# A spectral mixer on one core: single x tiles and a gated constant load in front, filter rows interleaved for one multiply per unit

## The chip, the cores and the metric

The kernel runs on one core of one Trainium2 chip. The metric is the time of the whole kernel on the device in microseconds, median of the runs. A profile of one execution comes with it; its span is a little shorter than the time (134.2 us against 136.11 us), since it leaves out what lies around the first and last instruction.

## The reference

Two blocks follow each other on x, 2048 by 512 in bf16. The first normalises x, takes a two-dimensional real Fourier transform, multiplies by a complex filter `w_r + i w_i` (2048 by 257), and transforms back. The second normalises again and applies a token-mixing MLP over the 2048 rows.

```python
def _A_ref(x, w_r, w_i):
    X = rfft2(x.astype(float32), axes=(-2, -1))
    X = X * (w_r + 1j * w_i)
    return irfft2(X, s=(S, D), axes=(-2, -1)).astype(bfloat16)

def _B_ref(x, w1, b1, w2, b2):
    h = _layernorm(x, axis=-1)
    u = gelu(einsum("bsd,sf->bdf", h, w1) + b1)      # F = 1376
    return (einsum("bdf,fs->bds", u, w2) + b2).transpose(0, 2, 1)

h  = x + _A_ref(_layernorm(x), A_w_r, A_w_i)
h2 = h + _B_ref(_layernorm(h), B_w1, B_b1, B_w2, B_b2)
```

## The kernel before

Row `16*p + s2` of x lies in partition `p` as tile `s2`, so x is 16 tiles of 128 by 512. The stages are:

1. front: statistics of each tile, first DFT matrices `FP` scaled by the tile's `1/std` into `FS` (so the normalisation is folded into the transform), matmuls `f1` on x, eviction to `Y`;
2. filter, in eight units `u` of four groups: `f2` (transform along the columns) to `CS`, `x` (the rest of the row transform) to PSUM, the multiply `v` by the filter rows `W` to `V`, and `g1` (start of the inverse) to `PQ`;
3. the rest of the inverse (`g2`, `g3`), the residual (`TT`, `H`), the second normalisation (`HH`);
4. the MLP, `mm1`, gelu and `mm2`.

A unit's multiply needs the `W` rows of its chunk: chunk 0 serves unit 0, chunk 1 units 1 to 3, chunk 2 units 4 to 7.

The instructions aren't written in order by hand. Each is declared with its engine, a priority and an assumed duration, and a list scheduler in Python picks the order for every engine before the program is built:

```python
st = max(eng_free[o.stream], o.dep_ready, avail, o.not_before)
key = (st, -o.prio, o.idx)          # earliest start first, then the higher priority
...
if o.is_dma:
    x0 = max(st + (3200.0 if st < 4000.0 else 1700.0), dma_free)
    dma_free = x0 + o.bytes / o.rate
    o.finish = dma_free + 200.0
```

The loads of the front, on the sync queue (SP) unless `"act"` is given, and the warm-up of TensorE:

```python
for q, (a, b) in enumerate(((0, 2), (2, 4), (4, 6), (6, 8), (8, 12))):
    ldx(a, b, 90 - q)               # x tiles a to b-1, 128 KB each
ldf(2, 84)                          # 4 tiles of FP, 256 KB
ldx(12, 16, 83)
ldf(3, 82)
ldf(0, 90, "act")
act("table", ..., ACT.Abs_reciprocal_sqrt, ..., prio=88)
ldf(1, 87, "act", 1800.0)
dma("ld_E", ...); dma("ld_MR", ...) # constants of the later stages
...
K.op("zt", "dve", lambda eng, bank: eng.memset(ZT[:, :], 0.0), ..., prio=60)
for w_ in range(N_WARM):            # N_WARM = 20, matmuls on zeros
    warm(f"warm{w_}", wu, 50, first=w_ == 0, occ=427.0 if w_ < 9 else 216.0)
# matmuls f1 have prio 14; 12 more warm matmuls (prio 13) stand after the first tiles
```

The statistics of tiles 1 and 3 are on ScalarE, those of the others on VectorE (`bn_stats`, `bn_aggr`). The scaling `FS` of nine tiles is on GpSimd, the rest on ScalarE and VectorE.

The filter rows and the multiply:

```python
add("W", [NP, 2, NG, LW], bf, rw)   # partition, w (real or imaginary), group, 257 columns
...
d = W[0:NP:2, w, g0:g0 + ng, :].rearrange("p g l -> p (g l)")      # plus rows, both components
dma(f"ld_wp{ch}_{w}", d, AP(dram, g0 * LW, [[64 * LW, 32], [0, 2], [1, ng * LW]]), ...)
for comp in range(2):                                             # minus rows, one component
    d = W[1 + 2 * comp::4, w, h0:h0 + nh, :]
    dma(f"ld_wm{ch}_{w}{comp}", d, AP(dram, (64 - h0) * LW, [[64 * LW, 32], [-LW, nh], [1, LW]]), ...)
# chunk 0 has one more transfer for each w; ld_w1 waits for the last load of chunk 2
...
for w in range(2):                  # stage_x, unit u; ng groups, nh = 2 in units 0 and 7
    wt  = W[:, w, g0 + h * ng:g0 + h * ng + ng, :]
    win = AP(wt, wt.offset + 1, [.., [LW, ng], [1, 2], [2, NP]])
    vout = V[:, g0 + h * ng:g0 + h * ng + ng, w, :]
    eng.tensor_tensor(vout, psum, win, ALU.mult)
```

Of the kernel before, what the change touches and what calls it, by code (L numbers as in the profile page):

```python
# [36 lines left out]
def _row(sign, comp, k2, s):  # L37
    return 4 * (k2 * 2 + s) + 2 * comp + sign
# [136 lines left out]
class Builder:  # L175
# [101 lines left out]
    def schedule(self):  # L277
# [14 lines left out]
        while len(order) < len(ops):  # L292
# [38 lines left out]
            if o.is_dma:  # L331
                x0 = max(st + (3200.0 if st < 4000.0 else 1700.0), dma_free)
                dma_free = x0 + o.bytes / o.rate
                o.finish = dma_free + 200.0
            else:
                o.finish = st + o.lat
# [86 lines left out]
def memory_layout():  # L423
# [26 lines left out]
    add("W", [NP, 2, NG, LW], bf, rw)  # L450
# [21 lines left out]
    add("tb", [NP, 8], f32, region(32))  # L472
    add("B1s", [NP, 16], bf, region(32))
# [17 lines left out]
def build_kernel(nc, A_x, A_w_r, A_w_i, B_w1, B_b1, B_w2, B_b2, out):  # L491
# [68 lines left out]
    def ldf(q, pr_, stream="sp", nb=0.0):  # L560
        sl = slice(4 * q, 4 * q + 4)
        dma(f"ld_FP{q}", FP[:, sl, :, :], cin["FP"][:, sl, :, :], 1 << 18, outs=[FP[:, sl, :, :]], prio=pr_, stream=stream, not_before=nb)

    for q, (a, b) in enumerate(((0, 2), (2, 4), (4, 6), (6, 8), (8, 12))):
        ldx(a, b, 90 - q)
# [3 lines left out]
    ldf(0, 90, "act")  # L569
    act("table", T["tb"][:, 0:1], EPS[:, 0:1], ACT.Abs_reciprocal_sqrt, 1, ins=[EPS[:, 0:1]], prio=88)  # L570
    ldf(1, 87, "act", 1800.0)
# [3 lines left out]
    for ch, (u0, u1) in enumerate(((0, 1), (1, 4), (4, 8))):  # L575
        g0, ng = 4 * u0, 4 * (u1 - u0)
        lst = []
        for w, dram in ((0, A_w_r), (1, A_w_i)):
            d = W[0:NP:2, w, g0:g0 + ng, :].rearrange("p g l -> p (g l)")
            lst.append(dma(f"ld_wp{ch}_{w}", d, bass.AP(dram.tensor, g0 * LW, [[64 * LW, 32], [0, 2], [1, ng * LW]]),  # L580
                           64 * ng * 514, prio=42 - ch, group=f"w{ch}"))
            h0, nh = (g0, ng) if g0 else (1, ng - 1)
            for comp in range(2):
                d = W[1 + 2 * comp::4, w, h0:h0 + nh, :]
                lst.append(dma(f"ld_wm{ch}_{w}{comp}", d, bass.AP(dram.tensor, (64 - h0) * LW, [[64 * LW, 32], [-LW, nh], [1, LW]]),
                               32 * nh * 514, prio=42 - ch, group=f"w{ch}", rate=300.0))
            if g0 == 0:
                d = W[1:NP:2, w, 0, :]
                lst.append(dma(f"ld_wz{ch}_{w}", d, bass.AP(dram.tensor, 32 * LW, [[64 * LW, 32], [0, 2], [1, LW]]),
                               64 * 514, prio=42 - ch, group=f"w{ch}", rate=300.0))  # L590
# [21 lines left out]
    ZT, BV = T["ZT"], T["bv"]  # L612
    K.op("zt", "dve", lambda eng, bank: eng.memset(ZT[:, :], 0.0), outs=[ZT[:, :]], occ=200.0, prio=60)  # L613
# [98 lines left out]
    def stage_x(u):  # L712
# [14 lines left out]
        for h in range(nh):  # L727
            for w in range(2):
                wt = W[:, w, g0 + h * ng:g0 + h * ng + ng, :]
                win = bass.AP(wt.tensor, wt.offset + 1, [list(wt.ap[0]), [LW, ng], [1, 2], [2, NP]])  # L730
                vout = V[:, g0 + h * ng:g0 + h * ng + ng, w, :].rearrange("p g (y j) -> p g y j", y=2)

                def tt(eng, bank, h=h, win=win, vout=vout):
                    s = psf[:, bank * 512 + h * 512:bank * 512 + h * 512 + 256 * ng].rearrange("p (g y j) -> p g y j", g=ng, y=2)
                    return eng.tensor_tensor(vout, s, win, ALU.mult)  # L735
                K.op(f"v_{u}_{h}{w}", "dve", tt, ins=[wt], outs=[vout], occ=50.0 + 1065.0 / nh, lat=170.0 + 1065.0 / nh, unit=unit, pr=True,
                     last=h == nh - 1 and w == 1, prio=11, after=wload[u])
# [93 lines left out]
    K.emit(es, ["dq_st"] + [f"dq_st_{s2}" for s2 in range(NS2 - 2, NS2)])  # L831
# [45 lines left out]
```

## Time and profile before

| what | before |
|---|---|
| time, median of 3 runs | 136.11 us (136.06 to 136.16) |
| span of the profile | 134.2 us |
| TensorE busy | 124.3 us, 93% |
| VectorE busy | 69.8 us, 52% |
| ScalarE busy | 63.9 us, 48% |
| GpSimd busy | 12.1 us, 9% |
| bytes moved | 22.16 MB in 12808 packets, 2592 of them under 512 B and 8736 under 2 KB |

In the profile PE is TensorE's matmuls and PEld its weight loads, DVE is VectorE, ACT ScalarE, POOL GpSimd. SPq and ACTq are the issues of transfers from the sync and the scalar engine. `L527` is the line of a helper that records every matmul, so matmuls are told apart by the tiles they read (`FS,X` is `f1`, `EM,Y` is `f2`, `CS,EM` is `x`, `EM,V` is `g1`). The chain of waits is followed back from the last instruction, at each step to what released it; time on it is what the end depends on. A row of the timeline has the start in us, the duration, the engine and the instruction, and in brackets how long the engine was idle before it and what it waited for. Rows of the timeline are merged, so one can hold several instructions (its `x` count).

### The profile page before, as it was taken

The numbers are of one execution on the slowest core, as the hardware profiler recorded it, in microseconds if no ns is written. First come the engines' busy times: TensorE is split into PE (matmuls) and PEld (weight loads), VectorE is DVE, ScalarE is ACT, GpSimd is POOL, SyncE is SP. The second block draws the span as 40 slices with busy tenths as digits, with TensorE's granted clock in tenths as the row PEclk, the third lists the DMA queues.
The fourth block names the chain that finished last, engine by engine and source line by source line (L and its number), as shares of the span: only waits on it lengthen the run. The fifth ranks groups of instructions, "written<-read, shape, count | busy, mean of one in ns | idle before, by whom it ended". The sixth has DMA issues, their size and how long they took to land.

```text
span 134.2 us, 2017 instructions
## 1 busy us (share of the span) xinstructions
PE 124.3 (93%) x776; PEld 74.4 (55%) x786; DVE 69.8 (52%) x137; ACT 63.9 (48%) x146; POOL 12.1 (9%) x33
## 2 busy tenths in 40 slices
PE   6979989998976979999999999999999999999991
PEld 2436656676845835654434444446666666666660
DVE  0379966999693799999981000000233242332422
ACT  4479976968955999995779622222000000000000
POOL 0198800006000000000000000000000000000000
PEclk9999999999999999999999999999999999999999
DMA  3999999989999999910000000000011212112121
GB/s 79 359 388 389 348 342 346 322 238 433 421 433 402 404 415 261 336 50 5 0 0 0 0 0 0 5 0 0 12 66 39 78 39 69 53 39 78 39 76 41
DMA packets 12808, 22.16 MB, mean 165 GB/s; under 512 B 2592, under 2 KB 8736, under 8 KB 12160
## 3 DMA queue, kind: packets, MB, share of 16 engines
q1 hardware_dynamic: 12512, 21.52, 45.0%
q10 hardware_dynamic: 288, 0.52, 1.4%
q8 instruction: 6, 0.10, 0.3%
q14 instruction: 2, 0.02, 0.0%
HBM read 19.95 MB, written 2.10 MB: 164 GB/s over the span
## 4 chain that ended last, share of the span: by engine, by line
PE 59%; DVE 24%; ACT 8%; DMA 5%; issue 1%; SPq 1%; ACTq 0%
PE ps L527 59%; DVE H L795 7%; ACT Y L545 5%; DMA X<-in_A_x_dram 5%; DVE TT L786 4%; DVE TT L788 4%; DVE HH L800 4%; DVE V L735 4%; ACT rs L545 1%; ACT PQ L545 1%; ACT FS L545 1%; DVE st L649 1%; SPq L517 1%; DVE OUT L825 1%; PE ps L617 0%
## 5 line engine op out<-in xcount | busy, mean ns | idle before, releaser
L527 PE MATMUL ps<-HH,W 128*128 128x512 bf16 (+1 forms) x173 | 40.4, 380 | 1.3 <-DVE HH L800 0.9
L527 PE MATMUL ps<-GT,W 128*128 128x512 bf16 (+1 forms) x172 | 37.9, 379 | 0.2
L825 DVE SCALAR_TENSOR_TENSOR OUT<-ps,B2f,H 128x512 bf16<-128x512 f32 x16 | 12.0, 751 | 48.7 <-PE ps L527 48.7
L527 PEld LDWEIGHTS ps<-GT,W 128*128 128x128 bf16 (+1 forms) x176 | 25.4, 144 | 12.7
L527 PEld LDWEIGHTS ps<-HH,W 128*128 128x128 bf16 (+1 forms) x176 | 17.2, 100 | 21.3 <-DVE HH L800 1.9
L735 DVE TENSOR_TENSOR V<-ps,W 128x1024 bf16<-128x1024 f32 (+1 forms) x20 | 18.5, 1001 | 1.9 <-PE ps L527 1.9
L545 ACT ACTIVATE GT<-ps,B1f 128x512 bf16<-128x512 f32 (+1 forms) x11 | 7.1, 688 | 14.6 <-PE ps L527 14.6
L545 ACT ACTIVATE JK<-H,nm 128x512 bf16<-128x512 bf16 x16 | 11.6, 724 | 3.0 <-DVE H L795 2.9
L527 PE MATMUL ps<-EM,V 128*128 128x128 bf16 x128 | 10.8, 220 | 1.2 <-DVE V L735 1.2
L649 DVE BATCH_NORM_STATS2 st<-X 128x6 f32<-128x512 bf16 x14 | 9.2, 666 | 5.1 <-DMA X<-in_A_x_dram 5.1
L545 ACT ACTIVATE PQ<-ps 128x512 bf16<-128x512 f32 x16 | 9.1, 596 | 4.3 <-PE ps L527 3.9
L617 PE MATMUL ps<-ZT 128*128 128x512 bf16 x32 | 9.4, 430 | 1.6 <-DVE ZT L613 1.2
L795 DVE TENSOR_TENSOR H<-ps,TT 128x512 bf16<-128x512 f32 x16 | 10.9, 683 | 0.0
L527 PE MATMUL ps<-EM,Y 128*128 128x256 bf16 x64 | 9.4, 274 | 0.7 <-ACT Y L545 0.4
L527 PEld LDWEIGHTS ps<-EM,V 128*128 128x128 bf16 x128 | 7.8, 98 | 3.9 <-DVE V L735 1.9
L527 PE MATMUL ps<-EM,PQ 128*128 128x256 bf16 x64 | 9.0, 273 | 0.8 <-ACT PQ L545 0.7
L545 ACT ACTIVATE EO<-ps 128x512 bf16<-128x512 f32 x16 | 9.2, 598 | 0.9 <-PE ps L527 0.9
L545 ACT ACTIVATE CS<-ps 128x512 bf16<-128x512 f32 x15 | 8.5, 602 | 2.3 <-PE ps L527 2.3
L527 PE MATMUL ps<-FS,X 128*128 128x256 bf16 x64 | 8.4, 274 | 1.0 <-POOL FS L629 0.8
L629 POOL TENSOR_SCALAR FS<-FP,rs 128x256 bf16<-128x256 bf16 x9 | 8.3, 935 | 0.9 <-ACT rs L545 0.9
L786 DVE TENSOR_TENSOR TT<-ps,X 128x256 f32<-128x256 f32 x16 | 6.7, 419 | 3.2 <-PE ps L527 3.2
L527 PEld LDWEIGHTS ps<-FS,X 128*128 128x128 bf16 x64 | 5.6, 97 | 4.1 <-POOL FS L629 2.6
(36 smaller groups left out, 79.6 us busy)
## 6 DMA issues: line engine op xcount, KB each, us to landing
W<-in_B_w_dram SPq DMA_DIRECT2D x4, 1376.0 KB, 11.4
W<-in_B_w_dram SPq DMA_DIRECT2D x10, 512.0 KB, 16.5
out_dram<-OUT SPq DMA_DIRECT2D x16, 128.0 KB, 1.7
X<-in_A_x_dram SPq DMA_DIRECT2D x4, 256.0 KB, 5.7
X<-in_A_x_dram SPq DMA_DIRECT2D x2, 512.0 KB, 7.5
EM<-c_EM SPq DMA_DIRECT2D x3, 256.0 KB, 8.3
W<-in_A_w_r_dram SPq DMA_DIRECT2D x1, 514.0 KB, 5.7
W<-in_A_w_r_dram SPq DMA_DIRECT2D x2, 257.0 KB, 6.2
```

The source lines that it names most:

```text
L517: return eng.dma_start(dst, src)
L527: return K.op(name, "pe", lambda eng, bank: eng.matmul(outf(bank), lhsT, rhs, start=start, stop=stop), ins=ins or [lhsT, rhs], occ=occ, la ...
L545: return eng.activation(dst, s, func, **kw)
L617: return K.op(name, "pe", lambda eng, bank: eng.matmul(ps[:, bank, :], ZT[:, 0:NP], ZT[:, :], start=True, stop=True), ins=[ZT[:, :]], occ= ...
L629: dve(f"fs{i}", lambda eng, bank: eng.tensor_scalar(FS[:, i, :, :], FP[:, i, :, :], rs, None, op0=ALU.mult), [FP[:, i, :, :], rs], [FS[:, ...
L649: dve(f"st_{i}", lambda eng, bank, i=i, x=x: eng.bn_stats(ST[:, i, 0:6], x), [x], [ST[:, i, 0:6]], 512, prio=25)
L735: return eng.tensor_tensor(vout, s, win, ALU.mult)
L786: dve(f"tl_{s2}", lambda eng, bank, tt=tt, xl=xl: eng.tensor_tensor(tt[:, 0, :], ps[:, bank, 256:512], xl, ALU.add), [xl], [tt[:, 0, :]], ...
L788: dve(f"th_{s2}", lambda eng, bank, tt=tt, xh=xh: eng.tensor_tensor(tt[:, 1, :], xh, ps[:, bank, 256:512], ALU.subtract), [xh], [tt[:, 1, ...
L795: return eng.tensor_tensor(hs.rearrange("p (h d) -> p h d", h=2), e, tt[:, :, :], ALU.add)
L800: dve(f"hh_{s2}", lambda eng, bank, s2=s2, hs=hs: eng.tensor_scalar(HH[:, s2, :], hs, NM[:, s2:s2 + 1], R2[:, s2:s2 + 1], op0=ALU.add, op1 ...
L825: dve(f"fin{s2}", lambda eng, bank, dst=dst, bia=bia, hs=hs: eng.scalar_tensor_tensor(dst, ps[:, bank, :], bia, hs, op0=ALU.add, op1=ALU.add),
```

## The change

The change has three parts.

The front: x tiles 0 and 1 come as single transfers of 128 KB, the later ones in pairs; the first DFT rows (`ld_FP0`) are issued only after a gate, a clear of a scratch tile on VectorE that does nothing else; the second DFT rows move from the scalar queue to the sync queue; and a transfer of 64 bytes out of the DFT constants is issued at once. It's meant to bring the first x tile sooner, with nothing beside it on the way.

The filter rows: `W` is laid out with real and imaginary rows of a group side by side, and the rows of a unit's partitions are reordered so that the component is the fastest index. Every transfer then carries rows of one component, 514 bytes at a time, in place of the plus rows of both components at once.

The multiply: with that layout one instruction multiplies PSUM, read twice, by both the real and the imaginary rows.

The scheduler's model of a transfer is changed with it, so the order of instructions may differ in other places too.

```diff
 def _row(sign, comp, k2, s):
-    return 4 * (k2 * 2 + s) + 2 * comp + sign
+    return 4 * (k2 * 2 + s) + 2 * sign + comp
...
-                x0 = max(st + (3200.0 if st < 4000.0 else 1700.0), dma_free)
-                dma_free = x0 + o.bytes / o.rate
+                x0 = max(st + (1750.0 if st < 900.0 else 2200.0), dma_free)
+                dma_free = x0 + o.bytes / (min(o.rate, 310.0) if x0 < 7000.0 else o.rate)
...
-    add("W", [NP, 2, NG, LW], bf, rw)
+    add("W", [NP, NG, 2, LW], bf, rw)
...
-    for q, (a, b) in enumerate(((0, 2), (2, 4), (4, 6), (6, 8), (8, 12))):
-        ldx(a, b, 90 - q)
+    gate = K.op("gate", "dve", lambda eng, bank: eng.memset(T["TT0"][:, :, :], 0.0), outs=[T["TT0"][:, :, :]], occ=560.0, prio=59)
+    for q, (a, b) in enumerate(((0, 1), (1, 2), (2, 4), (4, 6))):
+        ldx(a, b, 96 - q)
+    ldf(1, 88)
+    ldx(6, 8, 87)
+    ldx(8, 10, 86)
+    ldx(10, 12, 85)
     ldf(2, 84)
     ldx(12, 16, 83)
     ldf(3, 82)
-    ldf(0, 90, "act")
-    act("table", ..., prio=88)
-    ldf(1, 87, "act", 1800.0)
+    act("table", ..., prio=95)
+    dma("touch", T["pt"][0:1, :], cin["FP"][0:1, 0, 0, 0:32], 64, outs=[T["pt"][0:1, :]], prio=99, stream="act")
+    ldf(0, 90, "act", after=[gate])
...
-            d = W[0:NP:2, w, g0:g0 + ng, :].rearrange("p g l -> p (g l)")
-            lst.append(dma(f"ld_wp{ch}_{w}", d, bass.AP(dram.tensor, g0 * LW, [[64 * LW, 32], [0, 2], [1, ng * LW]]),
-                           64 * ng * 514, prio=42 - ch, group=f"w{ch}"))
             for comp in range(2):
-                d = W[1 + 2 * comp::4, w, h0:h0 + nh, :]
+                d = W[comp::4, g0:g0 + ng, w, :]
+                lst.append(dma(f"ld_wp{ch}_{w}{comp}", d, bass.AP(dram.tensor, g0 * LW, [[64 * LW, 32], [LW, ng], [1, LW]]),
+                               32 * ng * 514, prio=42 - ch, group=f"w{ch}", rate=300.0))
+                d = W[2 + comp::4, h0:h0 + nh, w, :]
...
-            for w in range(2):
-                wt = W[:, w, g0 + h * ng:g0 + h * ng + ng, :]
-                win = bass.AP(wt.tensor, wt.offset + 1, [list(wt.ap[0]), [LW, ng], [1, 2], [2, NP]])
+            wt = W[:, g0 + h * ng:g0 + h * ng + ng, :, :]
+            win = bass.AP(wt.tensor, wt.offset + 1, [list(wt.ap[0]), [LW, 2 * ng], [1, 2], [2, NP]])
+            s = bass.AP(s.tensor, s.offset, [list(s.ap[0]), [256, ng], [0, 2], [1, 256]])
+            return eng.tensor_tensor(vout, s, win, ALU.mult)
```

## The prediction, made before the change was run

> **What bounds the kernel now.** I read the page first, then the chain of waits in order of time, then the timeline of each stretch that the change touches. No engine bounds the whole span: TensorE is busy for 93% of it, but the chain gives it 59%, VectorE 24% and ScalarE 8%. So I split the span by the chain. These are six of its pieces (start us, duration us, what):
>
> ```profile
> 1.64 6.20 DMA X<-in_A_x_dram
> ...
> 17.52 1.47 ACT Y L545 x3
> ...
> 19.04 6.68 PE ps L527 x72
> ...
> 36.71 3.56 DVE V L735 x4
> ...
> 44.61 0.42 DVE TT L786
> ...
> 69.65 0.33 DVE HH L800
> ```
>
> The reader sees four stretches. To 19.04 us is the front: x arrives, is normalised, and goes through the first DFT. From 19.04 to about 42.5 is the filter, where VectorE multiplies by the filter rows and TensorE transforms on both sides. From 44.61 to 69.98 VectorE is the bound (25.33 us busy of 25.40 in the table of stages), and after that TensorE alone. The last two are untouched: whatever the change wins or loses must show as an earlier or later start of the first `TT`, now 44.61, and I carry that shift unchanged to the end.
>
> The timeline of the front:
>
> ```profile
> 1.17 5.81 PE L617 MATMUL ps<-ZT 128*128 128x512 bf16 x20 [1.17 <-DVE ZT L613]
> ...
> 5.14 0.69 DVE L649 BATCH_NORM_STATS2 st<-X 128x6 f32<-128x512 bf16 x1 [4.03 <-DMA X<-in_A_x_dram]
> 5.14 0.63 ACT L545 ACTIVATE JK<-X 128x512 bf16<-128x512 bf16 x1 [2.54 <-DMA X<-in_A_x_dram]
> ...
> 7.77 0.61 PE L527 MATMUL ps<-FS,X 128*128 128x256 bf16 x4 [0.79 <-POOL FS L629]
> ...
> 10.30 1.05 ACT L545 ACTIVATE Y<-ps 128x512 bf16<-128x512 f32 x2
> ```
>
> VectorE waits 4.03 us for the first x. The 20 warm-up matmuls end at 6.98 (1.17 + 5.81), 0.79 us before real work starts. From 10 to 18 us VectorE and ScalarE have no gap worth naming: the table of stages gives 2.00 of 2.00 for both in 10 to 12.
>
> VectorE in the filter stage, and the issues of the last filter chunk on the sync queue:
>
> ```profile
> 21.90 13.80 DVE L735 TENSOR_TENSOR V<-ps,W 128x512 bf16<-128x512 f32 x14 [0.93 <-PE ps L527]
> 36.71 4.75 DVE L735 TENSOR_TENSOR V<-ps,W 128x1024 bf16<-128x1024 f32 x6 [1.01 <-PE ps L527]
> ```
>
> ```profile
> 15.10 1.96 SPq L517 DMA_DIRECT2D W<-in_A_w_r_dram  x3
> 17.10 2.19 SPq L517 DMA_DIRECT2D W<-in_A_w_i_dram  x3
> ```
>
> Fourteen multiplies run without a gap for 13.80 us, so VectorE bounds here, with one hole of 1.01 us in which it waits for TensorE. No multiply waits for filter rows: the last of them lands 8.2 us after its issue at 18.6, at 26.8, and its first user starts at about 31.2 (the chain has a V piece end at 31.18).
>
> **What the Trainium skill says.** "DMA: Bandwidth & Descriptors", section "Queues, rings and completion order": an engine takes turns between the queues that have work, a packet at a time. The trace agrees: the first pair of x tiles on the sync queue (issued 0.72, 4.4 us to landing) and the first DFT rows on the scalar queue (issued 0.71, 4.2 us), 256 KB each, land together at 5.1 and 4.9. "VectorE: DVE Perf Modes", section "The perf-mode tier table": a `tensor_tensor` with a PSUM operand runs at one element per cycle. The trace agrees: 681 ns for 512 elements and 1215 ns for 1024, a slope of 1.04 ns per element, so merging two multiplies saves only the fixed part. "Perfetto Trace Analysis", section "DMA Optimizations": transfers under 2 KB carry a marked overhead, large ones saturate better. The trace points the same way: 406 GB/s in 10 to 11 us, mostly x and DFT rows, and 311 to 343 GB/s in 15 to 18 us, mostly filter rows, half of them in 514-byte pieces.
>
> **Part 1, the front.** Bytes begin to flow at about 2.2 us (97 GB/s in 2.0 to 2.4, 200 to 230 in the next three slices). Now 512 KB must share that flow before the first statistics can run. After, tile 0 goes alone, 128 KB: 0.6 us at 215 GB/s, and I allow 0.7 us for the slowest engine and the receipt (the bytes moved run ahead of those landed all through the front). It lands at about 3.5 us, tile 1 at about 4.0. The gate runs behind the 0.27 us clear of `ZT` and is twice as long by its bytes, so it ends near 1.65; the DFT rows issued then land near 5.0, as late as now, but they no longer delay x. Statistics of tile 0 (0.66 + 0.2 + 0.3) end at 4.7, and the scaling on GpSimd (0.95) at 5.9.
>
> TensorE does not profit fully. In the list scheduler ties on the start time go to the higher priority, and warm-up has 50 against 14, so all 20 warm-ups still come first and the first real matmul can start at 6.98: 0.79 us gained where the data gained 1.6. But then work is waiting. A 256-column matmul follows the last by (0.61 - 0.27) / 3 = 0.11 us, 64 of them take 7.2 us; the 12 later warm-ups, at (0.82 - 0.38) / 2 = 0.22 us, take 2.6. That gives 6.98 + 9.8 = 16.8 us for TensorE. ScalarE: the first `Y` moves from 10.30 to about 8.0 (two tiles of matmuls after 6.98), and its 8.7 us from there to 18.98 end at 16.7. VectorE: from 3.5, 14 statistics at 0.66 end at 12.7, so it has room. Adding the last eviction (0.6) to 16.8, the second transform starts at 17.3 instead of 19.04: **-1.7 us**. The added copy and memset lie in idle time; the 64-byte read is one issue of about 0.4 us on the scalar queue.
>
> **Part 2, the multiply.** Start to start a 1024 multiply takes 1.14 us and a 512 one 0.60 ((13.80 - 4 x 0.60) / 10 = 1.14). Slope 1.04 to 1.07 ns per element leaves about 0.07 us fixed. Twenty become ten: **-0.7 us** on VectorE. Dependencies stay, since the transform after it needs both halves anyway. TensorE is near the same pace: per unit 8 x 0.11 + 8 x 0.05 + 16 x 0.056 = 2.2 us against 2.28 on VectorE now and 2.21 after, so I count 0.4.
>
> **Part 3, the filter rows.** The sign-plus rows, now runs of 2 to 8 KB, become 514-byte pieces too, and 20 issues become 28. An issue of W takes 0.65 us now, whether large or small (3 in 1.96). The queue starts W at 5.82 now; three more issues in front make it about 7.45. Twelve issues for the first chunk reach 15.3, eight for the second 20.6, eight for the third 26.1. The first chunk lands about 17.5, before its use near 20.2. The second, 1.58 MB in 5.3 us, is paced by issue at 300 GB/s and lands at about 23; its user is ready near 22.4: a wait of about half a microsecond. For the third, 4.2 MB of W now take 13.0 us (landing of the second constant block at 13.8 to 26.8). With the large half at 400 GB/s (5.3 us), the small half runs at about 270; then 2.1 MB take 7.7 us and land near 30, against a user ready at 29.1 to 29.6. I count the fourth unit's start at 30.0 for 31.2 now. From there the last four units take 4 x 2.21 = 8.8 us; now they take 10.3 with the hole; TensorE, which runs ahead while VectorE waits, should fill most of that. V ends near 39.6 to 40.0 instead of 41.46.
>
> **Sum.** Front -1.7, multiply -0.4, waits for rows +0.6: -1.5, so 136.11 - 1.5 = 134.6 us. W1 is issued only after the last filter rows, so near 30.3 instead of 26.74; its first part then lands 6.2 to 9 us later, before 40, and is used at about 47.5 (49.2 now): hidden.
>
> **Rivals.** (a) The filter rows win: W lands at 31 to 33 because 514-byte pieces run slower without large ones between them. For it: the fall from 406 to 311 GB/s as they enter. Against: issue rate, not bytes, paces most of it. It would give 135.5 to 137.5. (b) The rows keep up (the small ones run at 300 or more and the large ones were not faster): both gains stand, and the hole closes: 132.9 to 133.5. (c) The front's gain is held back: x is not early because the first transfer has a start-up cost that splitting does not touch, or the order leaves GpSimd (9 scalings at 0.94 us) as the bound. For it: the slow first slices of flow. Then the front gives 0.8, and the time is 135.5 or above.
>
> **Range and chances.** The front is fairly safe at -1 to -2.3, the filter stage anywhere from -1 to +2. I take 133.2 to 136.6. Faster by over 2% needs under 133.4, that is rival (b) nearly whole: 0.2. Slower by over 2% needs 138.8, a much worse (a): 0.08. The rest, 0.72, lies within.
>
> **What would show it.** First statistics near 3.5 us for 5.14, first real matmul at 7.0 for 7.77, second transform at 17.3 for 19.04. Multiplies of 2048 elements near 2.28 us. V multiplies that wait for W, which none does now, by 0.3 to 1.5 us in all. First `TT` near 43.1. Wrong if x lands no earlier, if V waits for W by more than 3 us or not at all, or if the last two stretches change their length.

## The result and the profile after

The changed kernel takes 136.89 us (median; 136.71 to 137.05) against 136.10 us for the kernel before in the same session. The ratio is 1.0057, with an interval of 1.004 to 1.0075: a small loss where a gain of 1.5 us was forecast. The span of the profile went from 134.2 to 135.0 us.

Of the kernel before, the front's first scaling and its flow from 4 to 6 us (in such a row of the table of stages the last number is GB/s; the one ahead of it is the busy share of the DMA engines, which can pass 1 where packets overlap):

```profile
6.76 0.95 POOL L629 TENSOR_SCALAR FS<-FP,rs 128x256 bf16<-128x256 bf16 x1 [0.21 <-ACT rs L545]
...
4.00:6.00 2.00, 2.00 (x11) 0.93 (x10) 0.82 (x2) 0.86 (x3) 0.05 (x1) 1.00 1.06 396
```

Now the timeline of the changed kernel's front. The helper of the matmuls is now `L528`, the scaling `FS` is `L635`.

```profile
1.69 0.36 ACTq L518 DMA_DIRECT2D FP<-c_FP  x1
...
3.37 0.69 DVE L655 BATCH_NORM_STATS2 st<-X 128x6 f32<-128x512 bf16 x1 [1.72 <-DMA X<-in_A_x_dram]
...
7.51 0.94 POOL L635 TENSOR_SCALAR FS<-FP,rs 128x256 bf16<-128x256 bf16 x1 [2.82 <-DMA FP<-c_FP]
7.54 0.69 DVE L655 BATCH_NORM_STATS2 st<-X 128x6 f32<-128x512 bf16 x1 [3.27 <-DMA X<-in_A_x_dram]
...
8.51 0.39 PE L528 MATMUL ps<-FS,X 128*128 128x256 bf16 x2 [0.22 <-POOL FS L635]
...
21.34 2.13 PE L528 MATMUL ps<-EM,Y 128*128 128x256 bf16 x17 [0.47 <-ACT Y L546]
```

The first statistics start at 3.37 us in place of 5.14, so the single tile does what it is for. Then nothing follows from it. GpSimd waits 2.82 us for the first DFT rows and starts the first scaling at 7.51 us (6.76 before). VectorE waits another 3.27 us for the third x tile. The second transform starts at 21.34 us, 2.30 us later than the 19.04 of before. That splits in two: the first scaling starts 0.75 us later, and from there to the second transform it takes 13.83 us in place of 12.28, 1.55 us more.

The chain of waits of the changed kernel over the same stretch (start us, duration us, what):

```profile
1.69 5.66 DMA FP<-c_FP
...
19.32 0.69 DVE Y L694
20.01 0.20 DVE FS L635
...
20.26 0.41 PE ps L528 x2
...
20.69 0.60 ACT Y L546
```

The DFT rows, issued at 1.69, land 5.66 us later at 7.35. In the kernel before the same 256 KB took 4.2 us, and this transfer was not on the chain. At the other end the scaling of the last tile stands on VectorE behind an eviction of `Y`, and the second transform waits for both.

The filter, in VectorE's timeline and in the groups with each shape apart (count, busy us, mean ns):

```profile
24.15 17.81 DVE L741 TENSOR_TENSOR V<-ps,W 128x1024 bf16<-128x1024 f32 x10 [0.93 <-PE ps L528]
45.22 0.42 DVE L792 TENSOR_TENSOR TT<-ps,X 128x256 f32<-128x256 f32 x1 [3.27 <-PE ps L528]
```

```profile
L741 DVE TENSOR_TENSOR V<-ps,W 128x2048 bf16<-128x2048 f32 x6 | 13.3, 2282 | 0.0
...
L741 DVE TENSOR_TENSOR V<-ps,W 128x1024 bf16<-128x1024 f32 x4 | 4.7, 1218 | 0.9 <-PE ps L528 0.9
```

Here the change gains. The ten multiplies run 17.81 us without a hole; before, twenty of them and a hole took 19.56 (21.90 to 41.46). So the last multiply ends at 41.96, only 0.50 us late, the first `TT` is 0.61 us late, and that is what the time shows.

The issues of the filter rows on the sync queue:

```profile
8.02 3.92 SPq L518 DMA_DIRECT2D W<-in_A_w_r_dram  x6
...
24.26 3.50 SPq L518 DMA_DIRECT2D W<-in_A_w_i_dram  x4
```

They start at 8.02 us (5.82 before) and end at 27.8. The last chunk lands at 32.4; its first user starts at 33.01. No multiply waits for filter rows, but there is only 0.6 us to spare.

### The profile page after: what moved, and what is told of

Its sections match the earlier page's. It is cut to its first block, busy times and chain, and to the rows that moved or that the text cites. A ratio compares the mean times of both kernels' runs of the same rounds, so it can differ in the third digit from the quotient of the medians.

```text
span 135.0 us, 2023 instructions
## 1 busy us (share of the span) xinstructions
PE 124.9 (93%) x776; PEld 75.0 (56%) x786; DVE 70.0 (52%) x128; ACT 63.5 (47%) x146; POOL 12.3 (9%) x33
## 4 chain that ended last, share of the span: by engine, by line
PE 56%; DVE 32%; DMA 4%; POOL 2%; ACT 1%; issue 1%; ACTq 0%; DVEq 0%; POOLq 0%
PE ps L528 54%; DVE V L741 12%; DVE H L801 7%; DMA FP<-c_FP 4%; DVE TT L792 4%; DVE TT L794 4%; DVE HH L806 4%; PE ps L623 2%; POOL FS L635 1%; DVE OUT L831 1%; DVE Y L694 1%; ACT PQ L546 0%; ACT Y L546 0%; ACTq L518 0%; ACT L546 0%
## 5 line engine op out<-in xcount | busy, mean ns | idle before, releaser
L528 PE MATMUL ps<-HH,W 128*128 128x512 bf16 (+1 forms) x173 | 40.4, 380 | 1.3 <-DVE HH L806 0.9
L528 PE MATMUL ps<-GT,W 128*128 128x512 bf16 (+1 forms) x172 | 37.9, 380 | 0.2
L528 PEld LDWEIGHTS ps<-GT,W 128*128 128x128 bf16 (+1 forms) x176 | 25.3, 144 | 12.8
L528 PEld LDWEIGHTS ps<-HH,W 128*128 128x128 bf16 (+1 forms) x176 | 17.2, 100 | 21.2 <-DVE HH L806 1.9
L741 DVE TENSOR_TENSOR V<-ps,W 128x2048 bf16<-128x2048 f32 (+1 forms) x10 | 17.8, 1856 | 0.9 <-PE ps L528 0.9
L623 PE MATMUL ps<-ZT 128*128 128x512 bf16 x32 | 10.9, 479 | 1.5 <-DVE ZT L566 1.2
L528 PE MATMUL ps<-FS,X 128*128 128x256 bf16 x64 | 8.5, 274 | 2.0 <-POOL FS L635 1.6
L528 PE MATMUL ps<-EM,V 128*128 128x128 bf16 x128 | 9.3, 220 | 0.4 <-DVE V L741 0.4
L528 PE MATMUL ps<-EM,PQ 128*128 128x256 bf16 x64 | 9.0, 273 | 0.8 <-ACT PQ L546 0.7
L528 PEld LDWEIGHTS ps<-EM,V 128*128 128x128 bf16 x128 | 7.5, 98 | 2.5 <-issue 1.7
L528 PE MATMUL ps<-EM,Y 128*128 128x256 bf16 x64 | 8.4, 273 | 0.5 <-ACT Y L546 0.5
L635 POOL TENSOR_SCALAR FS<-FP,rs 128x256 bf16<-128x256 bf16 x9 | 8.4, 943 | 4.0 <-DMA FP<-c_FP 2.8
L528 PEld LDWEIGHTS ps<-FS,X 128*128 128x128 bf16 x64 | 5.6, 98 | 5.5 <-POOL FS L635 3.5
```

Of the source, the lines that this page charges most:

```text
L528: return K.op(name, "pe", lambda eng, bank: eng.matmul(outf(bank), lhsT, rhs, start=start, stop=stop), ins=ins or [lhsT, rhs], occ=occ, la ...
L623: return K.op(name, "pe", lambda eng, bank: eng.matmul(ps[:, bank, :], ZT[:, 0:NP], ZT[:, :], start=True, stop=True), ins=[ZT[:, :]], occ= ...
L635: dve(f"fs{i}", lambda eng, bank: eng.tensor_scalar(FS[:, i, :, :], FP[:, i, :, :], rs, None, op0=ALU.mult), [FP[:, i, :, :], rs], [FS[:, ...
```

## The experiments

All ratios are to the kernel before, run beside on the same chip. Times are medians which, as the ratios do, leave out runs over 1.5% above the fastest of their kernel. Kernels with the new front scatter more than the others (no_gate 136.08 to 138.58 us, the kernel before 135.93 to 136.34 in the same session), and in four profiles of this front (after, front_only, wide_touch, no_touch) the DFT rows land between 6.4 and 7.35 us. So a difference of under a microsecond in one landing is not read as an effect.

Every edit also passes through the scheduler. Where no order is said to be kept, that of the instructions may have changed with the edit.

One table of all runs, from their timelines; in us. "Distance" is from the first scaling to the second transform, "wait" is the time that multiplies waited for filter rows. A trace is of one run: those of no_touch (137.70 us), gate_fpq (135.32), after_fpq (136.25) and old_model_fpq (136.19) are of runs 0.5 to 1 us above the median.

| kernel | first scaling | second transform | distance | wait | last multiply ends | time |
|---|---|---|---|---|---|---|
| before | 6.76 | 19.04 | 12.28 | 0 | 41.46 | 136.1 |
| after | 7.51 | 21.34 | 13.83 | 0 | 41.96 | 136.89 |
| wv_only | 6.60 | 18.98 | 12.38 | 0 | 39.72 | 134.46 |
| rows_only | 6.56 | 19.13 | 12.57 | 0 | 41.54 | 136.00 |
| front_only | 7.06 | 20.90 | 13.84 | 0 | 43.26 | 137.96 |
| wv_split | 5.96 | 18.96 | 13.00 | 0 | 39.75 | 134.76 |
| wv_gate | 8.38 | 21.45 | 13.07 | 0 | 42.23 | 136.53 |
| no_gate | 6.06 | 19.89 | 13.83 | 1.04 | 41.74 | 136.73 |
| no_touch | 6.55 | 20.38 | 13.83 | 1.57 | 42.88 | 136.69 |
| wide_touch | 6.95 | 20.79 | 13.84 | 0.40 | 42.13 | 136.92 |
| fp0_on_sp | 6.01 | 19.84 | 13.83 | 1.96 | 42.81 | 137.65 |
| fp0_from_x | 5.64 | 19.57 | 13.93 | 2.09 | 42.51 | 137.40 |
| fp01_from_x | 5.75 | 19.59 | 13.84 | 0.56 | 40.96 | 135.87 |
| x_gated | 8.42 | 19.80 | 11.38 | 0.31 | 41.11 | 135.72 |
| wv_fpq | 6.44 | 18.53 | 12.09 | 0.22 | 39.52 | 134.32 |
| gate_fpq | 7.82 | 19.89 | 12.07 | 0 | 40.68 | 134.76 |
| after_fpq | 5.58 | 19.42 | 13.84 | 1.21 | 41.43 | 135.69 |
| old_model | 6.97 | 19.59 | 12.62 | 1.48 | 41.93 | 136.92 |
| wv_newmodel | 6.48 | 20.27 | 13.79 | 0 | 40.88 | 135.62 |
| old_model_fpq | 5.48 | 18.18 | 12.70 | 2.35 | 41.39 | 135.70 |

### Which part gains and which loses

wv_only is the kernel before with the new row layout, its loads and the merged multiply; front and scheduler model stay.

```diff
-    add("W", [NP, 2, NG, LW], bf, rw)
+    add("W", [NP, NG, 2, LW], bf, rw)
     # with the row order, the 28 loads and the merged multiply of after
```

> The kernel before with the filter rows and the merged multiply of after, and its own front. Theory 'the front lost it': the second transform starts at 19.0 us as before, the multiplies run without a gap or with one short wait for rows (chunk 2 issued about 1.6 us earlier than in after, so landing near 30.8 against a user ready near 30.8), and the first TT comes at 43.0 to 43.5 for 44.61: 134.5 to 135.0 us. Rival 'the rows lost it': the multiplies wait for rows by 1 us or more in all, and the time is 136.0 us or above.

134.46 us, 0.9871 (0.9856 to 0.9885). VectorE's and TensorE's timeline:

```profile
18.98 2.18 PE L527 MATMUL ps<-EM,Y 128*128 128x256 bf16 x17 [0.41 <-ACT Y L545]
...
21.84 17.88 DVE L735 TENSOR_TENSOR V<-ps,W 128x1024 bf16<-128x1024 f32 x10 [0.94 <-PE ps L527]
```

The front is as before, the multiplies have no hole and no wait. This half of the change alone beats both kernels.

front_only is the other half: the kernel before with the new front and the new scheduler model.

```diff
-    for q, (a, b) in enumerate(((0, 2), (2, 4), (4, 6), (6, 8), (8, 12))):
+    for q, (a, b) in enumerate(((0, 1), (1, 2), (2, 4), (4, 6))):
     # with gate, 64-byte read, new order of the loads and new model of a transfer
```

> The kernel before with the front of after (loads, gate, small read, scheduler model), and its own filter rows and multiplies. Theory 'the front lost it': the second transform starts at about 21.3 us as in after, nothing later makes up for it, and the time is 138.0 to 138.6 us. Rival 'the rows lost it' (the front is held back in after by the many more issues of rows behind it): the second transform at 19 or earlier and the time at most 136.1 us.

137.96 us, 1.0124 (1.0089 to 1.0158), second transform at 20.90. So the front loses 1.8 us, and the filter half gains 1.7. Together that is nothing, where the change loses 0.8: in the trace of after the DFT rows land 0.44 us later than in that of front_only, and so does the second transform start, and the interval of front_only is 0.9 us wide.

rows_only is wv_only with two multiplies per unit, on the new rows:

```diff
-    wt = W[:, g0 + h * ng:g0 + h * ng + ng, :, :]      # one multiply for both
+    for w in range(2):
+        wt = W[:, g0 + h * ng:g0 + h * ng + ng, w, :]  # one each
```

> The kernel before with the rows of after (28 loads of 514-byte pieces, new layout), but two multiplies a unit as before. Theory 'the multiply brings all of the gain': the stretch of multiplies takes 18.5 to 19.6 us (twenty fixed parts of 0.07 us again, perhaps the hole of 1 us too) for 17.88 merged, and the time is 135.2 to 136.3 us. Rival 'the new order of work brings it, not the merged instruction': 134.3 to 134.8 us.

136.00 us, 0.9995 (0.9986 to 1.0003). VectorE's timeline:

```profile
21.99 13.79 DVE L735 TENSOR_TENSOR V<-ps,W 128x512 bf16<-128x512 f32 x14 [0.94 <-PE ps L527]
36.80 4.74 DVE L735 TENSOR_TENSOR V<-ps,W 128x1024 bf16<-128x1024 f32 x6 [1.01 <-PE ps L527]
```

The hole of 1.01 us is back with two multiplies per unit. The rows in 514-byte pieces cost no time that can be measured behind the old front. They are hidden there, not free: the last chunk lands at 30.2 us in place of 26.7. The whole gain belongs to the merged multiply: 1.01 us of hole and 0.65 us of fixed parts (13.79 + 4.74 = 18.53 against 17.88). Why merging closes the hole was not tried.

### What in the front loses

wv_split gives wv_only the two single x tiles and nothing else of the front; VectorE's order stays, that of the other engines shifts with them.

```diff
-    for q, (a, b) in enumerate(((0, 2), (2, 4), (4, 6), (6, 8), (8, 12))):
+    for q, (a, b) in enumerate(((0, 1), (1, 2), (2, 4), (4, 6), (6, 8), (8, 12))):
```

> The kernel before with the filter rows and the multiply of after, and of its front only the first pair of x as two single transfers; the DFT rows are issued at once on the scalar queue, both. Theory 'the gate and the queue order lost it, the single tiles are harmless': tile 0 lands near 3.8 us, the second transform starts at 18.6 to 19.1 and the time is 134.2 to 134.7 us (134.46 with the pair). Rival 'the 1 KB pieces of single tiles lose it': the second transform starts at 19.5 or later and the time is 135 us or above.

134.76 us, 0.9893 (0.9878 to 0.9908). The first statistics start 0.4 us earlier (4.62 against 4.99), the first scaling 0.64 earlier, and the second transform at 18.96 in place of 18.98. An earlier first tile buys nothing by itself.

wv_gate gives wv_only the gate and nothing else. Both transfers of DFT rows on the scalar queue stand behind it.

```diff
+    gate = K.op("gate", "dve", ... memset(TT0) ..., prio=59)
-    ldf(0, 90, "act")
+    ldf(0, 90, "act", after=[gate])
```

> The kernel before with the filter rows and multiply of after, and of its front the gate alone: the first DFT rows wait for it on the scalar queue, x stays in pairs. Theory 'the gate moves the slow reads of the constants onto the path': the first DFT rows land at 6.5 us or later for 4.8, the second transform starts at 19.8 to 21 for 18.98, and the time is 135.2 to 136.3 us for 134.46. Rival 'the gate costs only its own delay' of 0.9 us, hidden behind the warm-up: second transform at 19.2 or earlier, 134.3 to 134.8 us.

136.53 us, 1.0035 (1.0012 to 1.0058): 2.07 us more than wv_only. Its timeline:

```profile
1.68 0.35 ACTq L517 DMA_DIRECT2D FP<-c_FP  x1
...
8.38 0.94 POOL L630 TENSOR_SCALAR FS<-FP,rs 128x256 bf16<-128x256 bf16 x1 [2.70 <-DMA FP<-c_FP]
...
9.84 1.29 DVE L650 BATCH_NORM_STATS2 st<-X 128x6 f32<-128x512 bf16 x2 [4.26 <-DMA X<-in_A_x_dram]
...
21.45 2.12 PE L527 MATMUL ps<-EM,Y 128*128 128x256 bf16 x17 [0.47 <-ACT Y L545]
```

The issue is 0.97 us later, the landing 3.3 us later (8.2 for 4.9 before), and x behind the first pairs is late too: VectorE waits 4.26 us for it. The gate with its consequences costs as much as the whole new front. Among these is another order of work on TensorE, VectorE, ScalarE and GpSimd, as the scheduler sees the later load; gate_fpq below keeps that order and stays within 0.3 us of wv_only, so the order alone isn't the loss.

no_gate takes the gate's wait out of after.

```diff
-    ldf(0, 90, "act", after=[gate])
+    ldf(0, 90, "act")
```

> After, with the first DFT rows issued at once on the scalar queue instead of behind the gate. Theory 'cold constants' (the first reads of the DFT constants are slow for about 3 us from wherever they start, and hold up the x packets on the same engines): the rows land near 5.0 to 5.5 us for 7.35, tiles 2 and 3 of x near 6 for 7.5, the second transform starts near 19.2 for 21.34. But chunk 2 of the filter rows landed at 32.4 in after, so the multiplies then wait for it, and the whole gains only 0.5 to 1.0 us on after: 135.9 to 136.4. Rival 'late issue' (the rows land late only since they are issued 1 us later): they land near 6.3 and the second transform starts near 20.3.

136.73 us, 1.0048 (1.0032 to 1.0064), with the order of all engines as in after. The rows, now issued at 1.29 behind the 64-byte read, land at 5.9. The second transform comes back by 1.45 us to 19.89, and almost none of that reaches the time. VectorE's timeline says where it goes:

```profile
25.46 6.69 DVE L741 TENSOR_TENSOR V<-ps,W 128x2048 bf16<-128x2048 f32 x3 [0.40 <-DMA W<-in_A_w_i_dram]
32.79 8.95 DVE L741 TENSOR_TENSOR V<-ps,W 128x2048 bf16<-128x2048 f32 x5 [0.64 <-DMA W<-in_A_w_i_dram]
```

Multiplies now wait for filter rows twice, and the last five start at 32.79, when the last chunk is there. In after the late front hid this wall.

no_touch leaves out the 64-byte read.

```diff
-    dma("touch", T["pt"][0:1, :], cin["FP"][0:1, 0, 0, 0:32], 64, ..., prio=99, stream="act")
```

> After, without the 64-byte read. Theory 'cold constants': the small read warms nothing that matters, so the first DFT rows land at 7.3 to 7.8 us as in after and the time is within 0.3 us of 136.9. Rival 'the small read does the harm': they land near 5 to 6 us and the time falls by 0.6 us. Rival 'the small read helps': they land 0.5 us later or more.

136.69 us, 1.0041 (1.0025 to 1.0056), its interval lies over that of after: the read does neither good nor harm.

### Why the DFT rows land so late

Bytes per time in the first stretches, GB/s, from the table of stages of each trace, and the landing of the first DFT rows:

| kernel | 2 to 4 us | 4 to 6 us | 6 to 8 us | rows issued, landed |
|---|---|---|---|---|
| before | 211 | 396 | 357 | 0.71, 4.9 |
| after | 188 | 244 | 328 | 1.69, 7.35 |
| wv_gate | 281 | 187 | 241 | 1.68, 8.2 |
| no_gate | 227 | 202 | 348 | 1.29, 5.9 |
| fp0_on_sp | 205 | 255 | 256 | 1.63, 5.85 |
| wide_touch | 204 | 203 | 298 | 1.68, 6.8 |
| x_gated | 213 | 285 | 368 | 0.71, 4.1 |
| gate_fpq | 239 | 292 | 380 | 1.68, 7.7 |
| after_fpq | 226 | 346 | 324 | 1.69, 5.4 |

The line of no_gate for 4 to 6 us:

```profile
4.00:6.00 2.00, 2.00 (x6) 0.73 (x5) 0.00 (x0) 1.43 (x5) 0.21 (x1) 1.00 0.85 202
```

With the gate the whole flow is slow from 4 to 6 us. It is as slow in no_gate, where the rows wait for nothing and yet go 0.58 us later than in the kernel before. So the gate isn't needed for it: with the constants as they were, every trace with the rows issued at 1.29 us or later has 187 to 255 GB/s there, and every trace with both rows and x issued at 0.71 or 0.72 has 365 to 396. Four tries at the reason:

fp0_on_sp: the rows come third on the sync queue, without gate, so that only one queue is at work.

```diff
     ldx(0, 1, 96); ldx(1, 2, 95)
+    ldf(0, 94)
-    ldf(0, 90, "act", after=[gate])
```

> After, with the first DFT rows on the sync queue, third in line after the two single x tiles, with no gate. Theory 'cold constants': the flow is still slow for about 3 us once these rows are read, so 4 to 6 us moves 200 to 270 GB/s and they land at 6 us or later. Rival 'cold queue or two queues at once': with one queue alone the flow reaches 390 GB/s by 4 us, and the rows land at 4.8 to 5.2 us.

137.65 us in one run; the rows land at 5.85, 4.2 us after their issue as in the kernel before, but the flow from 4 to 6 us is 255 GB/s. Slow with one queue as well, so turns between two queues are not needed for it.

wide_touch: the early read takes 64 bytes of each of the 128 rows of the constants.

```diff
-    cin["FP"][0:1, 0, 0, 0:32], 64
+    cin["FP"][:, 0, 0, 0:32], 8192
```

> After, with the small read widened from 64 bytes of one row to 64 bytes of each of the 128 rows (the rows are 8 KB apart, so it goes once over the whole of the constant). Theory 'cold constants, place by place' (each part of the constant is slow when first read): the early small reads take the slow part on themselves, the DFT rows issued behind the gate then land at 5.0 to 5.8 us for 7.35 and the second transform starts at 19.5 to 20.3. Rival 'any first load is slow whatever is read': no change beyond 0.5 us.

136.92 us, 1.006 (1.0042 to 1.0078), landing 6.8. A wider touch doesn't help either.

fp0_from_x and fp01_from_x fill the first quarter, or the first two quarters, of the DFT rows from x tiles 14 and 15 (and 12 and 13) instead of from the constants, so four or eight tiles are transformed with x bytes in place of DFT rows; the amount of work is the same.

```diff
-    ldf(0, 90, "act", after=[gate])
+    dma("ld_FP0", FP[:, 0:4, :, :], x_psd[:, 14:16, :], 1 << 18, ..., stream="act", after=[gate])
     # fp01_from_x: the second quarter from x_psd[:, 12:14, :] as well
```

> After, with the first gated transfer on the scalar queue reading 2 KB a partition out of x (tiles 14 and 15) in place of the first DFT rows, so that those rows hold the wrong numbers; sizes, queue and gate are kept. Theory 'cold constants' (it is the place read from): 2 KB pieces take about 84 ns from the start, 4 to 6 us moves 350 GB/s or more for 244, and the transfer lands at 5.5 us or earlier for 7.35. Rival 'cold queue or two queues at once' (it is the queue): the flow in 4 to 6 us stays near 200 to 260 GB/s and the transfer lands at 6.4 us or later.

> After, with the first two of the four DFT transfers reading out of x, so that eight tiles use wrong DFT rows; the first read of the constants beyond 64 bytes is then the third transfer, at about 9 to 11 us. Theory 'slow when first read, whenever that is': the third transfer's 2 KB pieces take over 110 ns on average and the flow falls under 300 GB/s for a stretch of 1 us or more after 8 us, where it is 390 or more in after. Rival 'only early in the run': flow of 380 GB/s or more from 4 us on throughout.

137.40 and 135.87 us, one run each. With the first quarter from x it lands at 5.5 and the flow holds 331 GB/s from 4 to 6 us, but falls to 179 from 6 to 8, while the second quarter is read from the constants. That looked as if the constants were slow at their first read. With both from x the flow is 303 GB/s from 4 to 6 us and 289 from 6 to 8, and no clear dip comes with the third quarter; neither reading was borne out.

x_gated turns wv_gate round: the DFT rows go at once, and the whole sync queue waits for the gate.

```diff
-    ldf(0, 90, "act", after=[gate])
+    ldf(0, 90, "act")
-    ldx(a, b, 90 - q)
+    ldx(a, b, 90 - q, after=[gate])   # as all other loads of the front on the sync queue
```

> Rows and multiply of after, with the gate the other way round: the DFT rows are issued at once on the scalar queue and the whole sync queue, x first, waits for the gate. Theory 'the constants are slow in their first reads': the slow stretch of about 2 us passes while x isn't yet asked for, the flow is 350 GB/s or more from 4.5 us on, and the first pair of x lands at 4.7 to 5.3 us, hardly later than the 4.9 without a gate. Rival 'whichever stream starts behind another is slow': the flow in 4 to 6 us falls to 200 to 270 GB/s and the first pair of x lands at 6.5 us or later.

135.72 us in one run. Read first and alone, the constants land 3.4 us after their issue, at 4.1. So being read for the first time doesn't by itself make them late. The flow is 285 GB/s from 4 to 6 us, between what either theory expected.

Another candidate is where the pieces lie. A quarter of the DFT rows is 2 KB out of every 8 KB in memory. In three kernels the constants are stored quarter by quarter, each a contiguous 256 KB, with everything else, the order of every engine too, unchanged:

```diff
-    c["FP"] = np.stack([-fp, fp], axis=2)
+    c["FP"] = np.stack([-fp, fp], axis=2).reshape(NP, 4, 4, 2, NP).transpose(1, 0, 2, 3, 4)
-    cin["FP"][:, sl, :, :], 1 << 18
+    cin["FP"][q], 1 << 18
```

> The kernel before with the filter rows and multiply of after, and the DFT constants stored quarter by quarter, so that each of the four transfers reads one contiguous 256 KB instead of 2 KB out of every 8 KB. Every instruction and its order is the same. Theory 'the pitch makes the first reads slow': the flow in 2 to 4 us rises from 214 to 300 GB/s or more, x and the first DFT rows land at about 4.2 us for 4.9, and the time falls to 133.8 to 134.3 us. Rival 'the constants are slow when first read, however they lie': flow and time as before within 0.3 us (134.2 to 134.7).

> The run with rows, multiply and the gate alone (wv_gate, 136.71 us), with the constants stored so that each transfer reads one contiguous 256 KB. Order of all instructions the same. Theory 'pitch': the first DFT rows land at 5.6 us or earlier for 8.2, the second transform starts at 19.5 or earlier for 21.45, and the time is 134.3 to 135.0 us. Rival 'it is not the pitch': rows at 7 us or later, second transform at 20.5 or later, 135.9 us or above.

> After as it is, with the constants stored so that each of the four transfers reads one contiguous 256 KB. Theory 'pitch': the first DFT rows land at 5.6 us or earlier for 7.35, and the time falls to 135.3 to 136.2 us, held there by chunk 2 of the filter rows. Rival 'it is not the pitch': within 0.3 us of 136.9.

wv_fpq 134.32 us, 0.9876 (0.9859 to 0.9892), as wv_only. gate_fpq 134.76 us, 0.9884 (0.9859 to 0.9909), 1.77 less than wv_gate. after_fpq 135.69 us, 0.9971 (0.9958 to 0.9985), 1.2 less than after. After's page and after_fpq's page count the same packets:

```profile
DMA packets 16939, 22.17 MB, mean 164 GB/s; under 512 B 2754, under 2 KB 13250, under 8 KB 16418
```

```profile
DMA packets 16939, 22.17 MB, mean 165 GB/s; under 512 B 2754, under 2 KB 13250, under 8 KB 16418
```

Only the addresses differ. So this layout of the constants costs 1.2 to 1.8 us of time where the rows come behind the gate (the old_model pair below, on one chip, differs by 1.22), and nothing that can be measured where they go first. A pitch by itself isn't enough: each pair of x tiles is 2 KB out of every 16 KB, and the quarter that fp0_from_x read in this way behind the gate landed at 5.5. The Trainium skill has a kin of this: "DMA: Bandwidth & Descriptors", section "Latency and other measured facts", tells of copies between tensors in memory whose rows lie a large power of two apart: they run at 207 GB/s with 512 KiB between rows and at 103 with 4 MiB, and it calls the mechanism an inference. A pitch of 8 KB isn't in it; these runs show an effect of the layout there, for 2 KB pieces read beside x, and not its mechanism. It isn't the whole of it: in gate_fpq the rows still land at 7.7 us, 6.0 after their issue, no clear change from wv_gate; there the time comes from the x tiles beside them (VectorE's wait for x is 1.99 us in place of 4.26). Why these rows stay late is open, and so is what the layout does in no_gate, where the flow was slow too: that pair was not run.

### The order of the front, and the wall behind it

In nine kernels with the new front and the new scheduler model the distance is 13.83 to 13.93 us, whatever lands when. In after_fpq the first scaling starts 1.18 us earlier than in the kernel before and the second transform 0.38 later. wv_newmodel puts only the new model into wv_only: the order on TensorE, VectorE and ScalarE changes, the issues and GpSimd's order stay.

```diff
-    x0 = max(st + (3200.0 if st < 4000.0 else 1700.0), dma_free)
-    dma_free = x0 + o.bytes / o.rate
+    x0 = max(st + (1750.0 if st < 900.0 else 2200.0), dma_free)
+    dma_free = x0 + o.bytes / (min(o.rate, 310.0) if x0 < 7000.0 else o.rate)
```

> wv_only with only the scheduler's model of a transfer replaced by that of after. Theory (the order is what lengthens the front): the second transform starts 13.5 to 14 us after the first scaling in place of 12.38, that is at 19.8 to 20.6, and the time is 135.2 to 136.2. Rival (the order by itself costs nothing): as wv_only, 12.2 to 12.6 us, 134.3 to 134.7.

135.62 us, 0.9959 (0.9944 to 0.9974), 1.16 us more than wv_only. Its timeline:

```profile
6.48 0.95 POOL L629 TENSOR_SCALAR FS<-FP,rs 128x256 bf16<-128x256 bf16 x1 [0.21 <-ACT rs L545]
...
19.19 0.61 PE L527 MATMUL ps<-FS,X 128*128 128x256 bf16 x4 [0.55 <-DVE FS L629]
...
20.27 2.13 PE L527 MATMUL ps<-EM,Y 128*128 128x256 bf16 x17 [0.47 <-ACT Y L545]
```

The first scaling is 0.12 us earlier than in wv_only, yet the second transform is 1.29 later. The last four `f1` matmuls wait for the last scaling on VectorE, which now stands behind two evictions of `Y` (it starts at 18.86; 17.16 in wv_only). The order alone costs this. It doesn't add up with the gate's cost: 2.07 and 1.16 us, where the whole front loses 1.8.

old_model takes the new model out of after, old_model_fpq out of after_fpq (the diff above reversed).

> After, with only the scheduler's model of a transfer put back to that of before: the same transfers, gate and multiplies, another order of the instructions. In all traces of the new front so far the second transform starts 13.83 to 13.93 us after the first scaling, whenever that was; in the kernel before 12.28. Theory (the new order lengthens the front by itself): the distance falls to 12.2 to 12.8, the second transform starts at 18.8 to 20.0 with the first scaling at 6.5 to 7.5, the time is 135.2 to 136.1, and multiplies wait for filter rows by up to 1 us. Rival (the single tiles and the late x lengthen it, whatever the order): the distance stays at 13.6 to 14, the time at 136.6 to 137.1.

> The after with the old model and with the constants stored quarter by quarter: both known causes of a late second transform gone. First scaling near 5.6 and the second transform at 17.9 to 18.4, near the 17.3 of the prediction, by the order theory. If then only the front counted, the time would be 134.0 to 134.5. If the filter rows are the second wall (last chunk near 32.5 us behind 11 issues of the front), multiplies wait 1.5 to 3 us for them, the last multiply ends near 41.4 and the time stays at 135.3 to 135.9.

136.92 us, 1.006 (1.0045 to 1.0076), and 135.70 us, 0.9971 (0.9956 to 0.9986): each as it was with the new model. The distance falls to 12.62 and 12.70 as the order theory says; the gain in time that it put on old_model stays away, for the filter rows take it, as the wall was expected to do in old_model_fpq. TensorE's and VectorE's timeline of old_model_fpq, its chain of waits up to 22 us, where the shares by line are, and its table of stages:

```profile
6.94 0.60 PE L528 MATMUL ps<-FS,X 128*128 128x256 bf16 x4
...
21.04 2.36 DVE L741 TENSOR_TENSOR V<-ps,W 128x1024 bf16<-128x1024 f32 x2 [0.94 <-PE ps L528]
25.58 6.69 DVE L741 TENSOR_TENSOR V<-ps,W 128x2048 bf16<-128x2048 f32 x3 [2.18 <-DMA W<-in_A_w_i_dram]
32.44 8.95 DVE L741 TENSOR_TENSOR V<-ps,W 128x2048 bf16<-128x2048 f32 x5 [0.17 <-DMA W<-in_A_w_i_dram]
```

```profile
by line: SPq L518 90.7%; issue 6.8%
```

```profile
14.00:18.00 4.00, 3.56 (x30) 2.37 (x27) 3.52 (x11) 4.00 (x11) 3.37 (x12) 1.00 0.47 106
18.00:22.00 4.00, 3.82 (x38) 2.51 (x39) 2.14 (x3) 2.40 (x5) 0.00 (x0) 1.00 1.00 260
22.00:26.00 4.00, 4.00 (x47) 3.25 (x47) 1.82 (x3) 3.24 (x7) 0.00 (x0) 1.00 0.98 231
26.00:30.00 4.00, 2.13 (x32) 1.46 (x31) 4.00 (x3) 1.12 (x4) 0.00 (x0) 1.00 1.11 304
```

This front is 3.16 us faster than after's, and VectorE gives 2.35 us of it back waiting for filter rows. The last five multiplies start at 32.44 (32.48 in after_fpq) and end 8.95 us later. The chain to them is the sync queue's issues, one after the other from 0.72 us to the last one at 27.13, and then the 5.28 us to its landing. The Trainium skill names this case in "Perfetto Trace Analysis", section "What 'DMA-bound' means": a kernel can be bound on the issuing sequencer, whose track is then solid with DMA slices. The trace agrees for the first part: 90.7% of the chain to 22 us is issues, and from 14 to 18 us the DMA engines are busy for 0.47 of the time. From 18 us on they are busy throughout and move 231 to 304 GB/s, where the kernel before moved 336 to 344 from 16 to 26.7 us with its longer pieces among them; the issues lengthen from 0.6 to 0.8 us. So the rate of the small pieces has a share in the last landing. How the wall divides between the two was not tried.

wv_only has the same 28 issues of filter rows and is clear of the wall, because its queue has fewer loads of the front ahead of them: it starts on the rows at 5.67 us and not at 8.02, and its last chunk lands at 30.0 and not at 32.4.

## Why the prediction was wrong

**x early: right.** First statistics 3.37 us (forecast 3.5), second tile 3.67 (4.0), gate done and rows issued at 1.69 (1.65).

**"The DFT rows issued then land near 5.0, as late as now, but they no longer delay x": the step that failed first.** They landed at 7.35, and the next x pair, at 7.54, was delayed all the same. The step moved the issue by 1 us and left the landing where it was. The runs show that a later issue of these rows is paid for more than once (wv_gate: issue +0.97, landing +3.3 us, time +2.07), partly because of how the constants lie in memory. The first scaling, forecast for 4.95 (5.9 less 0.95), came at 7.51, and the first real matmul, forecast for 6.98, at 8.51: 1.53 us of the miss at the second transform.

**The front's length: the second step that failed.** From the first real matmul to the second transform the prediction has 10.32 us, TensorE's work and a last eviction summed without a wait. It took 12.83: 2.51 us more, and 1.53 + 2.51 is the whole miss of 4.04 us (21.34 for 17.3). old_model_fpq tests this sum by itself: the first real matmul comes at 6.94 as forecast and the order is the old model's, yet 11.24 us pass (11.27 in the kernel before). So the sum was 0.9 us short in any case. Most of the other 1.6 us is the new scheduler model, which the prediction gave no cost at all: it lengthens the distance from the first scaling by 1.14 to 1.41 us (after_fpq and old_model_fpq, after and old_model, wv_newmodel and wv_only). Rival (c) saw that the front could gain less, to 0.8 us; that it could lose stood nowhere, and "the front is fairly safe at -1 to -2.3" cut the range short.

**The multiply: right in size, too low in effect.** 2282 ns for 2048 elements (forecast 2.28 us) and 0.65 us of fixed parts (0.7). Only 0.4 was counted, since TensorE was thought near the same pace; measured was 1.7 us, because the hole went too.

**The rows: right in kind, mis-sized, and hidden.** The first twelve issues took 0.65 us each as forecast, but started at 8.02 (7.45), and the last eight took 6.6 us (5.5, where eight times 0.65 is 5.2). They ended at 27.8 (26.1), and the last chunk landed 4.7 us behind them (3.9), at 32.4 (30). With the front as forecast, multiplies would have waited not 0.6 but some 2.3 us: old_model_fpq, whose second transform at 18.18 comes near the forecast 17.3, waits 2.35 and takes 135.70 us. So even a right front would have led to about 135.7 and not 134.6. That is rival (a), which reckoned with the rate of small pieces alone: of the 2.4 us by which the last chunk was late, some 1.7 are in the issues and the rest behind them. That the measured 136.89 lies in this rival's 135.5 to 137.5 is luck. In after no multiply waited at all, which the prediction had set down as a sign against it.

**The last two stretches: right.** The shift of the first `TT`, 0.61 us, is carried to the end, where the span has 0.8.

With the measured terms the sum is +2.30 for the front, -1.75 for multiply and hole, 0 for the rows: +0.55 us, against 0.61 at the first `TT`.

## What to carry to other kernels

An operand that is loaded first gains only if its partner doesn't come later for it: here both were needed for the first scaling, and delaying one cost more than the earlier other could bring. A change in a scheduler's cost model is a change of the kernel, to be timed by itself, and a small edit that the scheduler sees, as the gate was, can reorder other engines too. And when a front gets faster, look at when the next stage's loads are issued: the queue that issues them may already set the same end.

## What was not expected of the hardware

Delaying one 256 KB load by 1 us made it land 1.4 to 3.3 us later, and all loads together were slow (187 to 254 GB/s from 4 to 6 us, 396 before); at a delay of 0.58 us, in no_gate, the flow was as slow (202). The same bytes in the same number of packets, but contiguous and not 2 KB out of every 8, took 3.7 us in place of 5.66 in after, though not in gate_fpq (6.0). Why the layout shows behind the gate and not where the rows go first, and what else makes these loads late, stays open.
